# Start of a scan with feed-forward kernel: first unit's decay product moved ahead of the column product, five dummy matmuls left out, constant fills moved, weight block 0 loaded in two parts

## The chip, the core and the metric

The kernel runs on one core of one Trainium2 chip. The metric is the device time of one execution in microseconds; the time before is the median of three runs. A profiled execution has a time of its own, and a span from its first to its last instruction, which is a little shorter.

## What is computed

A state-space scan over 4 batches, 8 heads, 768 positions (head size 32, state size 16), and then a two-layer network over the 3072 tokens that come out of it:

```python
L = np.exp(cum[:, :, :, None] - cum[:, :, None, :]) * causal   # cum: running sum of log a
M = np.einsum('bhin,bhjn->bhij', Cc, Bc) * L
y = einsum(M, xc) + einsum(Cc, state) * np.exp(cum)
state = decay_full * state + sum_j(Bc_j * xc_j * decay_from_j)
...
h = x @ w_in          # 256 -> 2048
out = np.maximum(0.01 * h, h) @ w_out
```

All inputs are float32 and the output is float32.

## The kernel before

**Units.** The positions are cut into 8 chunks of 96 (`Q`). One chunk of one batch is a unit, `u = 4 * chunk + batch`, 32 in all, each with 8 heads. For a unit the kernel needs a decay matrix `lt` (112 rows: 96 positions and 16 rows of the incoming state; 8 heads by 96 columns), the scores `sc` of the unit (C times B), their elementwise product, and then the unit's products: `y` from `lt` and `xs` (line 348) and the new state from `xs` and `bn` (line 357).

**Decay matrices.** Units 0 and 1 (`DIRECT = 2`) get theirs in float32: `decay_mask` (line 239) puts large negative numbers above the diagonal into a PSUM tile `pd`, `decay_direct` (line 246) adds the sums of logarithms from `reach` (filled by GpSimd, line 199) through the matrix `after`, and `decay_of` (line 276, ScalarE) takes the exponential. Units 2 to 15 use a shorter way: the running sums are split into three bfloat16 parts on VectorE (`split_sums`, lines 227 to 230), stored to DRAM (`parts_d`), loaded back as rows of `dl` (line 254) and `dr` (line 257), and `decay_pe` (line 265) makes the matrix with one bfloat16 matmul for each half. `dl` also has rows that are constant: `upto_b` (copied by ScalarE, line 630), ones and zeros (set by VectorE, lines 611 and 612). `dr` is filled by lines 183, 187 and 191.

**Column product.** `columns` (line 217) makes the sums from a position to the chunk's end for all 256 columns of `la`, and ScalarE turns them into `erev` (line 218). `state_decay` (line 303, GpSimd) multiplies `bn` by it, and the state products of line 357 wait for that.

**Scores.** `scores(u)` works in two halves. Each half takes a PSUM tile `sc` of two banks from a pool of two tiles, runs its matmuls (line 321), and VectorE multiplies the result into `lt` (line 326). `columns` uses one of the two tiles of the same pool (`second`), the running sums another (`first`).

**Dummies.** `keep_warm` issues matmuls of an all-zero matrix (line 128) that nothing reads: `WARM = 6` at the start, `WARM2 = 2` behind the masks, `WARM2 = 2` ahead of the first `decay_pe`, and one ahead of each of `scores(2)`, `scores(3)` and `scores(4)`.

**Order.** The instructions of each engine stand in the order in which the program writes them (lines 597 to 689); each engine works in that order and waits on semaphores. The loop of line 638 runs over units 0 to 9: the decay matrix of unit `u + 2`, the scores of unit `u + 1`, the products of unit `u`, with VectorE's difference `xl` (line 391) for each unit behind them, and between them the decoding of weight blocks on ScalarE and VectorE (lines 445, 452, 458, 465, 472). Then the two-layer network begins: `ffn_in` (line 554) and `ffn_out` (line 578) run over 16 blocks of 128 hidden features and tiles of 512 tokens, with the units 10 to 31 put between them.

**Loads.** All loads are issued by SyncE in order, but for the first load of `dr` rows, which ScalarE issues. The order at the start is `la`, `bt`, two of `cc`, `bn`, `xs`, then (as soon as the parts are ready) the store `parts_d`, weight block 0 (`raw`, 512 KB), two loads of `dl` rows, a load of `dr` rows, and the loads of chunk 1.

Of the kernel before, what the change touches and what calls it, by code (L numbers as in the profile page):

```python
# [10 lines left out]
F32 = mybir.dt.float32  # L11
F32R = mybir.dt.float32r
BF16 = mybir.dt.bfloat16
U32 = mybir.dt.uint32
# [4 lines left out]
Q = 96  # L19
NC = S // Q  # L20
QE = Q + N
# [7 lines left out]
B_COLS = NB * QE  # L29
LAG = 3  # L30
WARM = 6
WARM2 = 2
RAWS = 3
SHIFT = 448
LOAD = 4
# [25 lines left out]
BUSY = (17, 21, 25, 30, 34, 38, 42, 46, 50)  # L61
LIGHT = (9, 11, 13, 14, 16)
KD = Q + 3 * NH + 3
MAG_MIN = float(np.uint32(0x38000000).view(np.float32))
MAG_MAX = float(np.uint32(0x47EFFFFF).view(np.float32))

# [2 lines left out]
def scan_ffn(ctx: ExitStack, tc: tile.TileContext, a_l, b_l, c_l, bn_l, x_l, w_l, out_l):  # L69
# [25 lines left out]

    raws, bcs, xss, bns = {}, {}, {}, {}

    def fetch_w(f, eng=nc.sync):
        raws[f] = wr.tile([128, 2 * DM, 2], U32, name="raw")
        eng.dma_start(raws[f].rearrange("p c w -> p (c w)"), w_l[f].bitcast(U32))  # L100

    ccs = [pst.tile([128, 2, NB, Q], F32, name=f"cc{i}") for i in range(2)]

# [99 lines left out]
        )  # L203

    nc.vector.tensor_copy(upto_b, upto)

    erev = const.tile([QE, ncols], F32, name="erev")
    ccol = const.tile([QE, ncols], F32, name="ccol")
# [388 lines left out]
    with tc.tile_pool(name="ps_d", bufs=2, space=PSUM, reuse_waits="tile") as ps_d:  # L597
# [10 lines left out]
        for u in range(DIRECT):  # L608
            fill_reach(u)
        nc.gpsimd.memset(ccs[1], 0.0)  # L610
        nc.vector.memset(dl[Q:], 1.0)
        nc.vector.memset(dl[Q:Q + 3 * NH, :, Q:], 0.0)
        fill_first()
        fill_less()
        prow = first[:, 0, :Q]
        sum_rows(prow, 0)
        split_sums(prow)
        nc.sync.dma_start(parts_d, parts)
        fetch_w(0)
        for u in range(DIRECT):  # L620
            decay_mask(pds[u])
        keep_warm(second[:, 1], WARM2)
        columns(erev, after, AF.Exp, second[:, 0])
        state_decay(0)
        decay_direct(0, pds[0])
        decay_of(0, pds[0])
        fill_slots(1, SLOTS // 2)
        scores(0)
        decay_direct(1, pds[1])
        nc.scalar.copy(dl[:Q], upto_b.unsqueeze(1).to_broadcast([Q, SLOTS, QE]))  # L630
        decay_load(DIRECT, 2, nc.scalar)
        decay_load(DIRECT + 2, SLOTS - 2)
        decay_of(1, pds[1])
        fill_slots(SLOTS // 2, SLOTS)
# [3 lines left out]
        for u in range(FIRST_UNITS):  # L638
            v = u + 2
            if u:  # L640
                decay_pe(v, free_tile())
            if u == 0:
                rest = unit_out(u, free_tile())
                rest()
            if u + 1 < FIRST_UNITS:
                scores(u + 1, int(0 < u < 4))
            else:
                pair_now((), (u + 1, u + 2))
                settle()
                state_decay(3)  # L650
                abs_more()
                pg = ctx.enter_context(tc.tile_pool(name="pg", bufs=LAG + 2))
                ffn_in(0, free_tile()[:, 0])
            if u:
                rest = unit_out(u, free_tile())
                rest()
            else:
                pd = free_tile()
                keep_warm(pd[:, 0], WARM2)
                decay_pe(v, pd)  # L660
            c, b = divmod(u, NB)
            if u == 1:
                fetch_w(1)
            if c + 2 <= 3:
                if b == 2:
                    fetch_bc(c + 2)
                if b == 3:
                    fetch_bn(c + 2)
            if u == 3:
                fetch_x(2)  # L670
            if u == 5:
                fetch_w(2)
            if u == 7:
                alloc_x(3)
                fetch_x(3)
            if u > 7:
                fetch_more()
            if u in (2, 5):
                state_decay(1 if u == 2 else 2)
            if u:  # L680
                settle()
            if u == 1:
                decode_abs(0)
            if u == 4:
                decode_abs(1)
            decode(LEAD.get(u, 0))
# [326 lines left out]
```

## Time and profile before

| What | Value |
|---|---|
| Runs | 318.66, 318.91, 316.94 us; median 318.66 us |
| Profiled execution | 318.41 us, its span 316.7 us |
| TensorE busy | 310.4 us (98%) |
| VectorE busy | 212.0 us (67%) |
| ScalarE busy | 180.7 us (57%) |
| GpSimd busy | 128.5 us (41%) |
| First matmul of the two-layer network (line 554) | starts at 29.24 us |

The profile names the engines PE (TensorE matmul), PEld (its weight loads), DVE (VectorE), ACT (ScalarE), POOL (GpSimd) and SP (SyncE); a `q` behind it is the engine's instruction queue. `L246` is line 246. Times count in us from the span's start. Matmuls are pipelined and their ends are modelled, so that a PE that waits can read as busy: a late start of the next group shows it. A float32 matmul shows as two records.

### The profile page before, as it was taken

The numbers are of one execution on the slowest core, as the hardware profiler recorded it, in microseconds if no ns is written. First come the engines' busy times: TensorE is split into PE (matmuls) and PEld (weight loads), VectorE is DVE, ScalarE is ACT, GpSimd is POOL, SyncE is SP. The second block draws the span as 40 slices with busy tenths as digits, with TensorE's granted clock in tenths as the row PEclk, the third lists the DMA queues.
The fourth block names the chain that finished last, engine by engine and source line by source line (L and its number), as shares of the span: only waits on it lengthen the run. The fifth ranks groups of instructions, "written<-read, shape, count | busy, mean of one in ns | idle before, by whom it ended". The sixth has DMA issues, their size and how long they took to land.

```text
span 316.7 us, 6261 instructions
## 1 busy us (share of the span) xinstructions
PE 310.4 (98%) x2407; PEld 245.8 (78%) x2407; DVE 212.0 (67%) x350; ACT 180.7 (57%) x353; POOL 128.5 (41%) x215
## 2 busy tenths in 40 slices
PE   8999999999999999999999999999999999999995
PEld 4566877777888878888887878788887888888884
DVE  5697787898987677767634444277367676767561
ACT  3776776848574755646454634375365547645551
POOL 6288644614554242724434330070035466335100
PEclk9999999999999999999999999999999999999999
DMA  6987626094518322350204101000001000000003
GB/s 166 253 223 232 173 81 214 23 274 133 155 67 248 108 89 66 96 126 2 90 0 156 66 1 68 0 2 0 0 0 66 2 0 0 2 0 0 2 2 132
DMA packets 11722, 26.29 MB, mean 83 GB/s; under 512 B 2380, under 2 KB 4652, under 8 KB 11692
## 3 DMA queue, kind: packets, MB, share of 16 engines
q1 hardware_dynamic: 11641, 25.88, 27.3%
q8 instruction: 19, 0.31, 0.4%
q14 instruction: 11, 0.09, 0.1%
q10 hardware_dynamic: 51, 0.01, 0.0%
HBM read 22.57 MB, written 3.32 MB: 82 GB/s over the span
## 4 chain that ended last, share of the span: by engine, by line
PE 95%; DVE 2%; ACT 1%; issue 1%; DVEq 0%; ACTq 0%
PE op L578 27%; PE hp L554 26%; PE sc L800 9%; PE op L820 7%; PE sc L820 6%; PE hp L800 3%; PE sc L411 3%; PE sc L348 3%; PE sc L321 2%; PE pd L348 1%; PE pd L265 1%; PE sc L128 1%; PE pd L246 1%; DVE w L465 1%; PE sc L357 1%
## 5 line engine op out<-in xcount | busy, mean ns | idle before, releaser
L567 DVE TENSOR_TENSOR gl<-hp,gh 128x512 fp32r<-128x512 f32 x63 | 43.4, 689 | 55.4 <-ACT hp L564 55.3
L561 ACT ACTIVATE gh<-hp 128x512 fp32r<-128x512 f32 x63 | 37.6, 598 | 63.0 <-PE hp L554 62.9
L578 PE MATMUL op<-gh,wh 128*128 128x512 f32 x128 | 50.9, 398 | 0.0
L554 PE MATMUL hp<-xh,wh 128*128 128x512 f32 x126 | 50.0, 397 | 0.4 <-DVE gl L567 0.4
L578 PE MATMUL op<-gh,wl 128*128 128x512 f32 x128 | 49.9, 390 | 0.0
L578 PE MATMUL op<-gl,wh 128*128 128x512 f32 x128 | 49.8, 389 | 0.0
L554 PE MATMUL hp<-xl,wh 128*128 128x512 f32 x126 | 49.2, 390 | 0.0
L554 PE MATMUL hp<-xh,wl 128*128 128x512 f32 x126 | 49.2, 390 | 0.0
L384 POOL COPY xs<-stage 16x64 f32<-16x64 f32 x112 | 30.8, 275 | 30.5 <-ACT stage L381 25.9
L766 POOL TENSOR_TENSOR sl<-s,sh 128x512 fp32r<-128x512 f32 x8 | 10.4, 1295 | 71.3 <-ACT sh L765 71.3
L564 ACT ACTIVATE hp<-hp 128x512 f32<-128x512 f32 x63 | 37.5, 595 | 0.0
L297 POOL TENSOR_SCALAR_AFFINE_SELECT lt<-lt 96x768 f32<-96x768 f32 x16 | 15.7, 982 | 47.8 <-ACT lt L296 47.8
L288 POOL TENSOR_TENSOR lt<-lt,ccol 112x768 f32<-112x768 f32 x16 | 25.2, 1577 | 10.8 <-DMA lt<-crow_d 6.0
L578 PEld LDWEIGHTS op<-gh,wh 128*128 128x128 f32 x128 | 24.0, 188 | 7.0 <-issue 1.4
L554 PEld LDWEIGHTS hp<-xh,wh 128*128 128x128 f32 x126 | 23.7, 188 | 5.9 <-DVE gl L567 0.8
L578 PEld LDWEIGHTS op<-gl,wh 128*128 128x128 f32 x128 | 24.0, 188 | 5.1
L554 PEld LDWEIGHTS hp<-xl,wh 128*128 128x128 f32 x126 | 23.6, 188 | 5.4 <-DVE xl L391 0.5
L578 PEld LDWEIGHTS op<-gh,wl 128*128 128x128 f32 x128 | 24.0, 188 | 4.6
L554 PEld LDWEIGHTS hp<-xh,wl 128*128 128x128 f32 x126 | 23.7, 188 | 4.8 <-DVE wl L485 0.2
L424 DVE TENSOR_TENSOR lt<-sc,lt 112x384 f32<-112x384 f32 x44 | 21.6, 548 | 3.5 <-ACT xh L386 1.8
L833 DVE TENSOR_TENSOR gl<-c,gh 128x512 fp32r<-128x512 f32 x24 | 23.1, 962 | 1.0 <-ACT c L830 0.7
L829 ACT ACTIVATE gh<-hp 128x512 fp32r<-128x512 f32 x8 | 4.8, 600 | 27.2 <-PE hp L800 27.2
(164 smaller groups left out, 617.0 us busy)
## 6 DMA issues: line engine op xcount, KB each, us to landing
raw<-w_l SPq DMA_DIRECT2D x16, 512.0 KB, 3.3
lt<-crow_d SPq DMA_DIRECT2D x16, 336.0 KB, 4.6
xs<-x_l SPq DMA_DIRECT2D x8, 384.0 KB, 8.2
out_l<-ob SPq DMA_DIRECT2D x12, 256.0 KB, 2.2
bn<-bn_l SPq DMA_DIRECT2D x8, 231.0 KB, 3.8
bt<-b_l SPq DMA_DIRECT2D x8, 224.0 KB, 6.4
cc<-c_l SPq DMA_DIRECT2D x16, 96.0 KB, 4.6
la<-a_l SPq DMA_DIRECT2D x1, 96.0 KB
```

The source lines that it names most:

```text
L288: nc.gpsimd.tensor_tensor(out=lts[u], in0=lts[u], in1=ccol[:, u * NH:(u + 1) * NH].unsqueeze(2).to_broadcast([QE, NH, Q]), op=ALU.subtract,)
L297: nc.gpsimd.affine_select(out=lt[:Q], in_=lt[:Q], pattern=[[0, NH], [1, Q]], compare_op=ALU.is_ge, fill=0.0, base=0, channel_multiplier=-1,)
L384: nc.gpsimd.tensor_copy(to[:, :, hh], stage[hh * D:hh * D + N])
L424: nc.vector.tensor_tensor(out=heads, in0=spaces[half][:QE, :, 2 * Q * e:2 * Q * (e + 1)], in1=heads, op=ALU.mult,)
L554: nc.tensor.matmul(hp, lhsT=w_half[half][:, f, k * 128:(k + 1) * 128], rhs=x[t][:, k, :], start=(n == 0), stop=(n == 5),)
L561: nc.scalar.activation(ghs[s], hp, AF.Prelu, alpha=0.01)
L564: nc.scalar.activation(hps[s], hps[s], AF.Prelu, alpha=0.01)
L567: nc.vector.tensor_tensor(out=gls[s], in0=hps.pop(s), in1=ghs[s], op=ALU.subtract)
L578: nc.tensor.matmul(op, lhsT=w_half[half][:, f, DM + m * 128:DM + (m + 1) * 128], rhs=x, start=(first and i == 0), stop=(last and i == 2),)
L800: nc.tensor.matmul(bank, lhsT=w[h], rhs=x[g], start=start and i == 0, stop=i == 2, skip_group_check=True,)
L820: nc.tensor.matmul(outs[t][m], lhsT=w_half[half][:, f, DM + m * 128:DM + (m + 1) * 128], rhs=x, start=first and i == 0, stop=last and i == 2,)
L833: nc.vector.tensor_tensor(out=gl, in0=g, in1=gh, op=ALU.subtract)
```

## The change

Seven things are edited at the start of the program; from the tenth unit on the program is the same.

1. `decay_direct(0)` and `decay_of(0)` stand right behind the masks, and `columns` behind them; ScalarE's load of `dr` rows is issued between the exponential of unit 0 and `erev`.
2. The two dummies behind the masks, the two ahead of the first `decay_pe` and the one ahead of `scores(4)` are left out.
3. `fill_slots(1, 4)` (VectorE) is written ahead of `decay_direct(0)`.
4. The ones and zeros of `dl` are set ahead of the clamp of `la`; the ones are written as float32 words that hold two bfloat16 ones each, half as many elements.
5. ScalarE's copy of `upto_b` into `dl` is ahead of the exponential of unit 0.
6. Weight block 0 is loaded in two halves of 256 KB, one ahead of the first load of `dl` rows, one behind it.
7. For unit 0, VectorE's difference `xl` (`rest()`) is written behind `scores(1)`; it stood ahead of it.

```diff
-    def fetch_w(f, eng=nc.sync):
-        raws[f] = wr.tile([128, 2 * DM, 2], U32, name="raw")
-        eng.dma_start(raws[f].rearrange("p c w -> p (c w)"), w_l[f].bitcast(U32))
+    def fetch_w(f, half=None):
+        if f not in raws:
+            raws[f] = wr.tile([128, 2 * DM, 2], U32, name="raw")
+        part = slice(0, 2 * DM) if half is None else slice(half * DM, (half + 1) * DM)
+        nc.sync.dma_start(
+            raws[f][:, part].rearrange("p c w -> p (c w)"),
...
     nc.vector.tensor_copy(upto_b, upto)
+    nc.vector.memset(dl[Q:].rearrange("p b j -> p (b j)").bitcast(F32), ONES)
+    nc.vector.memset(dl[Q:Q + 3 * NH, :, Q:], 0.0)
...
         nc.gpsimd.memset(ccs[1], 0.0)
-        nc.vector.memset(dl[Q:], 1.0)
-        nc.vector.memset(dl[Q:Q + 3 * NH, :, Q:], 0.0)
         fill_first()
         fill_less()
+        nc.scalar.copy(dl[:Q], upto_b.unsqueeze(1).to_broadcast([Q, SLOTS, QE]))
         prow = first[:, 0, :Q]
         sum_rows(prow, 0)
         split_sums(prow)
         nc.sync.dma_start(parts_d, parts)
-        fetch_w(0)
+        fetch_w(0, 0)
         for u in range(DIRECT):
             decay_mask(pds[u])
-        keep_warm(second[:, 1], WARM2)
+        fill_slots(1, SLOTS // 2)
+        decay_direct(0, pds[0])
+        decay_of(0, pds[0])
+        decay_load(DIRECT, 2, nc.scalar)
         columns(erev, after, AF.Exp, second[:, 0])
         state_decay(0)
-        decay_direct(0, pds[0])
-        decay_of(0, pds[0])
-        fill_slots(1, SLOTS // 2)
         scores(0)
         decay_direct(1, pds[1])
-        nc.scalar.copy(dl[:Q], upto_b.unsqueeze(1).to_broadcast([Q, SLOTS, QE]))
-        decay_load(DIRECT, 2, nc.scalar)
+        fetch_w(0, 1)
         decay_load(DIRECT + 2, SLOTS - 2)
...
             if u == 0:
                 rest = unit_out(u, free_tile())
-                rest()
             if u + 1 < FIRST_UNITS:
-                scores(u + 1, int(0 < u < 4))
+                scores(u + 1, int(0 < u < 3))
...
             else:
-                pd = free_tile()
-                keep_warm(pd[:, 0], WARM2)
-                decay_pe(v, pd)
+                rest()
+                decay_pe(v, free_tile())
```

**Order on PE around the scores of unit 0.** The first piece is the kernel before, behind the masks; `sc_159` is the tile of the column product, `pd_157` and `pd_158` those of the decays of units 0 and 1, `sc_189` and `sc_193` the two halves of `scores(0)`. What stands in brackets is the engine or load queue on which a row waits.

```order
L128 MATMUL sc_159<-idle_97 128x512
L217 MATMUL sc_159<-la_108,after_122 112x256 [waits Pool_49]
L246 MATMUL pd_157<-lt_127,after_122 112x384 [waits Pool_49]
L321 MATMUL sc_189<-cc0_95,bt_110 112x192 [waits DMAHW2_49,DMAHW1_49,DMAHW3_49,DVE_49,PE_49]
L321 MATMUL sc_193<-cc0_95,bt_110 112x192 [waits Activation_49]
L246 MATMUL pd_158<-lt_128,after_122 112x384 [waits Pool_49]
L348 MATMUL pd_214<-lt_186,xs_114 32x96 [waits DMAHW5_49,DVE_49]
```

The second piece is the same place in the changed kernel (its line 255 is line 246 of before, 226 is 217, 330 is 321, 357 is 348); `sc_190` and `sc_194` are the two halves of `scores(0)`.

```order
L255 MATMUL pd_159<-lt_127,after_122 112x384 [waits Pool_49]
L226 MATMUL sc_161<-la_108,after_122 112x256
L330 MATMUL sc_190<-cc0_95,bt_110 112x192 [waits DMAHW2_49,DMAHW1_49,DMAHW3_49,DVE_49,PE_49]
L330 MATMUL sc_194<-cc0_95,bt_110 112x192 [waits DVE_49]
L255 MATMUL pd_160<-lt_128,after_122 112x384 [waits Pool_49]
L357 MATMUL pd_213<-lt_183,xs_114 32x96 [waits DMAHW5_49,Activation_49]
```

The decay product of unit 0 has moved ahead of the column product. The second half of the scores waited on ACT before (for `erev`, which reads `sc_159`, whose banks `sc_193` takes over); now it waits on DVE, for the multiplication of the first half, because the built program gives `sc_194` the banks of `sc_190`.

**Order on DVE around unit 1.** First the kernel before, from the multiplications of unit 0 on; `pd_214` is the product tile of unit 0, `lt_204` the decay matrix of unit 1.

```order
L326 TENSOR_TENSOR lt_186<-sc_193,lt_186 112x384 [waits PE_49]
L191 COPY dr_126<-dr_126 120x3072
L391 TENSOR_TENSOR xl_232<-pd_214,xh_231 128x2x96 [waits PE_49,Activation_49]
L326 TENSOR_TENSOR lt_204<-sc_241,lt_204 112x384 [waits PE_49]
L326 TENSOR_TENSOR lt_204<-sc_245,lt_204 112x384 [waits PE_49]
```

Then the changed kernel at the same place (its lines 335, 198 and 400 are 326, 191 and 391 of before); `pd_213` is the product tile of unit 0, `lt_203` the decay matrix of unit 1.

```order
L335 TENSOR_TENSOR lt_183<-sc_194,lt_183 112x384 [waits PE_49]
L198 COPY dr_126<-dr_126 120x3072
L335 TENSOR_TENSOR lt_203<-sc_239,lt_203 112x384 [waits PE_49,Activation_49]
L335 TENSOR_TENSOR lt_203<-sc_243,lt_203 112x384 [waits PE_49]
L400 TENSOR_TENSOR xl_231<-pd_213,xh_230 128x2x96 [waits Activation_49]
```

The difference of unit 0 now stands behind both multiplications of unit 1. In both kernels the second `decay_pe` (unit 3) writes into the banks of the product tile of unit 0, and its first matmul waits on DVE for this difference.

**Order on PE ahead of the first `decay_pe`.** The kernel before, from the second half of `scores(1)` to the second `decay_pe`:

```order
L321 MATMUL sc_245<-cc0_95,bt_110 112x192 [waits PE_49]
L128 MATMUL pd_249<-idle_97 128x512 [waits Activation_49]
L265 LDWEIGHTS dl_125 [waits DMAHW0_49]
L265 MATMUL pd_249<-dr_126,dl_125 112x384 [waits DMAHW2_49]
L265 MATMUL pd_256<-dr_126,dl_125 112x384 [waits DVE_49]
L128 MATMUL sc_261<-idle_97 128x512 [waits DVE_49]
```

And the changed kernel (its lines 274 and 135 are 265 and 128 of before):

```order
L330 MATMUL sc_243<-cc0_95,bt_110 112x192 [waits PE_49]
L274 LDWEIGHTS dl_125 [waits DMAHW0_49,DMAHW1_49]
L274 MATMUL pd_248<-dr_126,dl_125 112x384 [waits Activation_49]
L274 MATMUL pd_253<-dr_126,dl_125 112x384 [waits DVE_49]
L135 MATMUL sc_258<-idle_97 128x512 [waits PE_49]
```

The two dummies into `pd_249` are gone; the first `decay_pe` itself now waits for the loads of `dl` and `dr` and, on ACT, for the exponential of unit 1.

More of the change, by code (lines that the diff above doesn't have):

```diff
@@ L31 @@
 WARM = 6
-WARM2 = 2
 RAWS = 3
@@ L63 @@
 KD = Q + 3 * NH + 3
+ONES = float(np.uint32(0x3F803F80).view(np.float32))
 MAG_MIN = float(np.uint32(0x38000000).view(np.float32))
@@ L96, in scan_ffn @@
     raws, bcs, xss, bns = {}, {}, {}, {}
-    def fetch_w(f, eng=nc.sync):
-        raws[f] = wr.tile([128, 2 * DM, 2], U32, name="raw")
-        eng.dma_start(raws[f].rearrange("p c w -> p (c w)"), w_l[f].bitcast(U32))
+    def fetch_w(f, half=None):
[4 more added lines that the diff above has]
+            raws[f][:, part].rearrange("p c w -> p (c w)"),
+            w_l[f].bitcast(U32).rearrange("p (c w) -> p c w", w=2)[:, part].rearrange(
+                "p c w -> p (c w)"
+            ),
+        )
     ccs = [pst.tile([128, 2, NB, Q], F32, name=f"cc{i}") for i in range(2)]
```

## The prediction

> **What bounds the kernel now.** I read the page first (span, chain that ended last), then the busy time by stage, then the timeline of the first 20 us, since only there the program changes. From the page:
>
> ```profile
> span 316.7 us, 6261 instructions
> PE 95%; DVE 2%; ACT 1%; issue 1%; DVEq 0%; ACTq 0%
> ```
>
> The stages (columns: stage, its length, then busy us and instructions of PE, PEld, DVE, ACT and POOL, granted clock, DMA share, GB/s):
>
> ```profile
> 5.00:10.00 5.00, 5.00 (x23) 2.45 (x21) 3.00 (x7) 2.13 (x3) 2.25 (x3) 1.00 0.74 221
> 20.00:25.00 5.00, 4.91 (x97) 3.12 (x96) 4.96 (x14) 4.26 (x11) 4.50 (x11) 1.00 0.78 220
> 30.00:316.70 286.70, 281.85 (x1972) 228.63 (x1971) 189.24 (x294) 161.26 (x313) 108.70 (x162) 1.00 0.23 70
> ```
>
> After 30 us PE is busy 281.85 of 286.7 us and does the same work in both kernels: whatever the start wins or loses is carried to the end as it is. From 20 to 25 us DVE is the full engine too (4.96 of 5 us). In 5 to 10 us PE reads 5.00 of 5, but only 23 instructions: there a late start counts, not the share. So the question is how much sooner or later the first units run. The timeline (start, length, engine, line, tiles, count, idle time before and its releaser):
>
> ```profile
> 4.20 1.49 PE L239 MATMUL pd<-later,upto_b 96*112 96x384 bf16 x4
> 5.48 0.93 PE L128 MATMUL sc<-idle 128*128 128x512 bf16 x2
> 6.24 0.60 PE L217 MATMUL sc<-la,after 96*112 96x256 f32 x2
> 6.68 1.45 PE L246 MATMUL pd<-lt,after 96*112 96x384 f32 x4
> 8.06 0.59 PE L321 MATMUL sc<-cc,bt 32*112 32x192 f32 x8
> 8.16 0.81 ACT L276 ACTIVATE lt<-pd 112x768 f32<-112x768 f32 x1 [0.91 <-PE pd L246]
> 8.58 1.54 PE L246 MATMUL pd<-lt,after 96*112 96x384 f32 x4
> 9.01 1.02 DVE L326 TENSOR_TENSOR lt<-sc,lt 112x384 f32<-112x384 f32 x2 [1.93 <-ACT lt L276]
> 10.16 0.81 ACT L276 ACTIVATE lt<-pd 112x768 f32<-112x768 f32 x1 [0.23 <-PE pd L246]
> 10.65 0.59 PE L321 MATMUL sc<-cc,bt 32*112 32x192 f32 x8
> 11.18 0.60 PE L128 MATMUL pd<-idle 128*128 128x512 bf16 x2
> 11.33 0.36 DVE L391 TENSOR_TENSOR xl<-pd,xh 128x192 fp32r<-128x192 f32 x1 [0.43 <-PE sc L321]
> 11.66 0.81 PE L265 MATMUL pd<-dr,dl 123*112 123x384 bf16 x4
> 12.24 1.51 ACT L276 ACTIVATE lt<-pd 112x768 f32<-112x768 f32 x2 [0.94 <-PE pd L265]
> 12.31 0.38 PE L128 MATMUL sc<-idle 128*128 128x512 bf16 x1
> 12.62 0.64 PE L321 MATMUL sc<-cc,bt 32*112 32x192 f32 x8
> 13.32 1.02 DVE L326 TENSOR_TENSOR lt<-sc,lt 112x384 f32<-112x384 f32 x2 [0.70 <-PE sc L321]
> 13.80 0.50 PE L265 MATMUL pd<-dr,dl 123*112 123x384 bf16 x2
> ```
>
> The reader is to see four things. DVE's first multiplications (9.01) waited 1.93 us for the exponential of unit 0 (8.16 to 8.97), and that for the decay product of line 246, ahead of which stand two dummies and the column product, 5.48 to 6.68. Both halves of `scores(0)` ran together at 8.06, ahead of that exponential. Both `decay_pe` (x4 at 11.66) ran back to back, because unit 0's difference `xl` (11.33) came early. And four masks take 5.48 - 4.20 = 1.28 us, 0.32 each, while four products of the same 384 columns take 12.31 - 11.66 = 0.65, 0.16 each: TensorE runs at half pace first. The dummy pair takes 0.76 (5.48 to 6.24), where a half-paced one takes 0.43 (512 columns against 384) and a full-paced one half of that; so the second dummy is part slow, and the pace doubles near 6.14.
>
> **The change, part by part.** *First unit's decays.* The product now starts at 5.48, 1.20 earlier. Before, the exponential started 8.16 - 6.68 = 1.48 after it. Of the four records one now falls into the slow time and takes 0.64 for 0.32, so it starts at 5.48 + 1.48 + 0.32 = 7.28 and ends at 8.09: 0.88 sooner than 8.97. The column product follows at about 7.18 and takes 0.44 (6.24 to 6.68), so the scores can start at 7.62, not 8.06.
>
> *The halves of the scores.* Here the order turns it round. The second half now goes into the banks of the first, so it waits until DVE has multiplied the first half. From scores to multiplication takes 13.32 - 12.62 = 0.70, so the first multiplication starts at 7.62 + 0.70 = 8.32 (the exponential has ended by then). One takes 0.55:
>
> ```profile
> L326 DVE TENSOR_TENSOR lt<-sc,lt 112x384 f32<-112x384 f32 x20 | 10.2, 550 | 3.0 <-ACT lt L276 1.9 <-PE sc L321 1.1
> 17.25 1.02 DVE L326 TENSOR_TENSOR lt<-sc,lt 112x384 f32<-112x384 f32 x2
> 17.88 1.02 PE L321 MATMUL sc<-cc,bt 32*112 32x192 f32 x8
> 18.18 0.35 DVE L391 TENSOR_TENSOR xl<-pd,xh 128x192 fp32r<-128x192 f32 x1
> ```
>
> In the pair at 17.25 PE resumes on a freed tile 17.88 - 17.80 = 0.08 behind the first multiplication's end. So the second half starts at 8.32 + 0.55 + 0.08 = 8.95. Queued behind it on PE is the decay product of unit 1, 0.52 later (8.06 to 8.58): 9.47, where it was 8.58. **The term is +0.89**: a gain of 0.88 on ScalarE has become a loss of 0.89 on PE. With lags 0.1 shorter in all it would be +0.79.
>
> *The first `decay_pe` and the difference.* With 0.89 added, `scores(1)` starts at 10.65 + 0.89 = 11.54, and the exponential of unit 1 ends at 10.16 + 0.89 + 0.81 = 11.86. The two dummies at 11.18 are gone, 0.48 (to 11.66), so unit 2's `decay_pe` can start at 12.06. But unit 3's waits for unit 0's `xl`, now behind both multiplications of unit 1: these start at 11.54 + 0.70 = 12.24, `xl` 0.93 later (17.25 to 18.18) at 13.17, and ends 0.36 later, 13.53; PE goes on at 13.61. Before, that product started at 11.66 + 0.32 = 11.98. **Lateness now: +1.63**; the 0.48 of the dummies has gone into this wait. Behind it on PE stand `scores(2)` and the products of unit 1, and behind these unit 4's `decay_pe`, 1.82 later as before (11.98 to 13.80), at 15.43; unit 3's exponential, 0.81 long and begun 12.24 - 11.66 = 0.58 behind its product, has ended by 15.0 and does not add. With lags 0.1 shorter at both places the sum is +1.43.
>
> *The dummy ahead of `scores(4)`* (about 0.3 with its change of weights, 12.31 to 12.62 for its like). It gains 0 to 0.3. I take 0.1: the next scores (17.88) are released by DVE's multiplication at 17.25, with DVE full in the stage that follows, so PE would only arrive sooner at that wait.
>
> *Fills and copies.*
>
> ```profile
> 2.81 0.29 DVE L602 TENSOR_SCALAR la<-la 96x256 f32<-96x256 f32 x1 [0.68 <-DMA la<-a_l]
> 3.34 0.81 DVE L611 MEMSET dl<- 32x896 bf16 x1 [0.24 <-issue]
> 4.22 0.11 DVE L612 MEMSET dl<- 24x64 uint32 x1
> 9.00 0.94 ACT L630 COPY dl<-upto_b 96x896 bf16<-96x896 bf16 x1
> ```
>
> DVE waited 0.68 for `la` ahead of the clamp. The memsets go there: 0.40 if the time goes with the elements (448 for 896), with the zeros 0.51; covered. If the ones took their 0.81 still, 0.92 with the zeros, the clamp and all behind would be 0.24 late: bounds 0 to +0.24, I take 0, since it is the same operation on half as many elements. The copy of `upto_b`, 0.94, lies in ScalarE's idle time ahead of 7.28. Taking them out of 3.34 to 4.33 lets the parts end about 0.2 sooner; who waits for them is the next part.
>
> *Loads and `erev`.*
>
> ```profile
> 5.84 0.35 SPq L618 DMA_DIRECT2D parts_d<-parts  x1
> 6.88 0.38 ACT L218 ACTIVATE erev<-sc 112x256 f32<-112x256 f32 x1 [2.47 <-PE sc L217]
> 7.34 1.06 POOL L303 TENSOR_TENSOR bn<-bn,erev 112x512 f32<-112x512 f32 x1 [1.15 <-ACT erev L218]
> 7.78 0.75 SPq L254 DMA_DIRECT2D dl<-parts_d  x2
> 8.23 0.51 ACTq L257 DMA_DIRECT2D dr<-parts_d  x1
> 8.94 0.36 SPq L106 DMA_DIRECT2D bt<-b_l  x1
> ```
>
> SyncE went on at 7.78, when the parts had landed. ScalarE's load of `dr` now waits for that too and not for the exponential, so it is issued near 7.8, 0.4 sooner, and its first user is PE at 12.06, not 11.66: 0.8 more room. `erev` is queued behind this issue on ScalarE: 7.8 + 0.51 = 8.3, ended at 8.7; `state_decay` (1.06) ends at 9.85, and PE needs it for the state products, behind unit 1's decay product (from 9.47, 1.54 long) and before 11.54: covered by about 1. The extra issue on SyncE is about 0.4, so chunk 1's loads are issued from 9.4, not 8.94; their first user, `scores(4)`, stands behind the `decay_pe` that was at 13.80 and is now later. Cost 0 (if ever one landed late, at most these 0.4).
>
> **Sum:** +0.89 + 0.74 (from 0.89 to 1.63) - 0.1 = **+1.5 us** on the profiled execution's 318.41 (span 316.7 and 1.7 around it): 319.9. The median of the runs, 318.66, is 0.25 above that execution; I leave the sum on the profiled one. Own range 319.2 to 320.7.
>
> **Rivals.** (1) *The lead comes through, faster.* The chain of waits shows PE without a gap through this stage:
>
> ```profile
> 5.69 0.72 PE sc L128 x2
> 11.24 0.54 PE pd L128 x2
> 16.15 0.22 PE sc L128
> ```
>
> If it were bound by its own work, each dummy left out would shorten it: 0.72 + 0.54 + 0.22 = 1.48, so 316.9. For it: the chain, and the 1.93 us that DVE waited. Against: the halves share banks. It decides only if the second half can start by 8.06, which needs the first multiplication to end by 7.98, 0.9 before my working has it. (2) *Nothing is left, 318.4.* DVE's full stage could take up the lateness. Against: DVE still waited 0.70 for PE at 13.32, so its queue starts later as a whole; the waits would have to be 1.5 shorter. (3) *The clock falls back, slower.* With the dummies gone PE stands still near 8.2 to 8.95 and 12.4 to 13.6; if that makes it run at half pace again for as long as the first time (from the first dummy to 6.14, about 5 us), half of that time's work is lost, 2.5 more: 318.4 + 1.5 + 2.5 = 322.4. For it: the slow pace at the start is in the rows, and the profile's clock column reads 1.00 in all stages, so it shows no fall beforehand. Against: these are 2.0 us in two pieces, of the 8.1 from 5.48 to 13.6; the rest is work.
>
> [...]
>
> **How the numbers follow.** Forecast 0.62; rival 1 0.14; rival 2 0.16; rival 3 0.08. Predicted 319.9. The range takes in rivals 1 and 2 and the forecast's upper end with both bounds (+0.24 and +0.4) put on: 316.8 to 321.4, leaving out rival 3 and little else. One per cent (3.2 us) is about what a measurement of this kernel can tell from no change. Rival 1 gives 0.5%, so faster by over 1% is 0.02; slower by over 1% is rival 3 with most of its weight, 0.06; within 1% 0.92.
>
> **What would show it.** In the profile after: exponential of unit 0 near 7.3; `scores(0)` in two groups of four, the second near 8.9 and released by DVE; unit 1's decay product near 9.4; two `decay_pe` apart, the second near 13.5 and released by `xl`; the first network matmul 1.2 to 1.7 later than before. It is wrong if both halves run together, if unit 3's `decay_pe` follows unit 2's at once, or if the half pace returns behind 8 us.

## The result and the profile after

| Kernel | Runs | Lowest | Median | Highest |
|---|---|---|---|---|
| before | 20 | 316.86 us | 318.12 us | 319.20 us |
| changed | 20 | 319.29 us | 325.91 us | 329.96 us |

The 20 runs of the changed kernel lie in separate places: seven at 319.29 to 319.96, two at 321.36 and 323.04, eleven at 325.63 to 329.96; one more run on record, 319.38, lies with the seven. The ratio to before is 1.0067, with a 95% interval of 1.0043 to 1.0091; it leaves out the eleven, as runs that lie over 1.5% above the kernel's fastest. The seven have a median of 319.65; forecast was 319.9. But the eleven are more than half, and before never shows such a thing: in the 66 runs that it had beside the experiments on the same chips its highest is 319.46. So the change has two effects: some 1.5 us in its best runs, and 1.7 to 10.3 us more in 13 of the 20. The second is a clock effect wherever a profile or the mean clock tells, the third rival of the prediction, which I had given a chance of 0.08.

The profiled execution of the changed kernel is one of the eleven (326.52 us). Its page and its stages (columns as before: stage, its length, busy us and instructions of PE, PEld, DVE, ACT, POOL, granted clock, DMA share, GB/s):

```profile
span 324.8 us, 6255 instructions
PE 90%; DVE 5%; ACT 2%; issue 1%; POOL 1%; DVEq 0%; ACTq 0%; POOLq 0%
```

```profile
5.00:10.00 5.00, 5.00 (x13) 2.48 (x11) 2.67 (x4) 1.67 (x3) 1.40 (x3) 1.00 0.56 172
20.00:25.00 5.00, 5.00 (x89) 3.03 (x85) 2.68 (x6) 2.41 (x7) 1.35 (x6) 1.00 0.09 17
```

The share of PE on the chain falls from 95% to 90%, and DVE's rises from 2% to 5%. From 5 to 10 us PE is still fully busy, but with 13 instructions instead of 23; and from 20 to 25 us DVE, full before (4.96), has 2.68. PE is busy and gets little done. The timeline of the same execution says why:

```profile
4.31 1.49 PE L248 MATMUL pd<-later,upto_b 96*112 96x384 bf16 x4
5.15 1.04 DVE L238 CAST parts<-rest 128x96 bf16<-128x96 f32 x1
5.38 0.73 POOL L619 MEMSET cc<- 128x768 f32 x1
5.59 2.77 PE L255 MATMUL pd<-lt,after 96*112 96x384 f32 x4
8.40 0.81 ACT L285 ACTIVATE lt<-pd 112x768 f32<-112x768 f32 x1 [2.92 <-PE pd L255]
9.14 0.98 PE L330 MATMUL sc<-cc,bt 32*112 32x192 f32 x4
10.25 0.56 DVE L335 TENSOR_TENSOR lt<-sc,lt 112x384 f32<-112x384 f32 x1 [2.51 <-PE sc L330]
10.86 0.98 PE L330 MATMUL sc<-cc,bt 32*112 32x192 f32 x4 [0.74 <-DVE lt L335]
11.78 2.90 PE L255 MATMUL pd<-lt,after 96*112 96x384 f32 x4
16.55 0.89 PE L274 MATMUL pd<-dr,dl 123*112 123x384 bf16 x2
18.07 0.80 PE L274 MATMUL pd<-dr,dl 123*112 123x384 bf16 x2 [0.63 <-DVE xl L400]
24.10 0.53 PE L274 MATMUL pd<-dr,dl 123*112 123x384 bf16 x2
37.15 0.50 PE L563 MATMUL pd<-xh,wh 128*128 128x512 f32 x1
```

The decay products take 2.77 and 2.90, where before's took 1.45 and 1.54; a `decay_pe` takes 0.89 at 16.55 and 0.53 at 24.10. TensorE ran at half pace until about 24 us, where before had it only to 6.14. The clock column of the stages reads 1.00 all the same: it holds what was recorded, and the first record of this execution is the grant, at 23.75; the half pace ahead of it is seen in the durations only (2.77 and 2.90 for 1.45 and 1.54). The first network matmul comes at 37.15, where it was 29.24: 7.91 later, and the execution is 326.52 - 318.41 = 8.11 longer. So the loss is made at the start and carried to the end, as the prediction had it.

Both predicted waits are there too: `scores(0)` in two groups of four, the second released by DVE (0.74), and two `decay_pe` apart, the second released by `xl` (0.63). To read them at full pace, the changed kernel was profiled once more:

> The changed kernel itself, once more, for a profile in which the clock is granted early. Theory: if it is, exp of unit 0 near 7.3, the second half of scores(0) near 8.95 and released by VectorE, unit 1's decay product near 9.5, unit 3's decay_pe near 13.6 and released by the difference, and a time of 319.3 to 320.0. If the clock is late again: the rows as in the profile after, near 325.9.

This execution took 322.98. Its clock came at 4.06, went at 14.30 and came back at 24.54, so it is at full pace from 4.06 to 14.30:

```profile
4.85 1.45 PE L255 MATMUL pd<-lt,after 96*112 96x384 f32 x4
4.99 1.21 DVE L238 CAST parts<-rest 128x96 bf16<-128x96 f32 x1
6.34 0.81 ACT L285 ACTIVATE lt<-pd 112x768 f32<-112x768 f32 x1 [0.86 <-PE pd L255]
6.40 1.35 DVE L198 COPY dr<-dr 120x2304 bf16<-120x2304 bf16 x1
6.67 0.58 PE L330 MATMUL sc<-cc,bt 32*112 32x192 f32 x4
7.66 0.55 DVE L335 TENSOR_TENSOR lt<-sc,lt 112x384 f32<-112x384 f32 x1
8.26 0.58 PE L330 MATMUL sc<-cc,bt 32*112 32x192 f32 x4 [1.02 <-DVE lt L335]
8.76 0.38 ACT L227 ACTIVATE erev<-sc 112x256 f32<-112x256 f32 x1 [1.60 <-DMA parts_d<-parts]
8.78 1.54 PE L255 MATMUL pd<-lt,after 96*112 96x384 f32 x4
9.22 2.01 POOL L312 TENSOR_TENSOR bn<-bn,erev 112x512 f32<-112x512 f32 x1 [3.10 <-ACT erev L227]
9.37 0.95 DVE L198 COPY dr<-dr 120x3072 bf16<-120x3072 bf16 x1
11.29 0.33 PE L366 MATMUL pd<-xs,bn 96*32 96x32 f32 x16 [0.50 <-POOL bn L312]
11.55 0.59 PE L330 MATMUL sc<-cc,bt 32*112 32x192 f32 x8
12.07 0.53 PE L274 MATMUL pd<-dr,dl 123*112 123x384 bf16 x2
13.58 0.48 PE L274 MATMUL pd<-dr,dl 123*112 123x384 bf16 x2 [0.98 <-DVE xl L400]
```

The two waits are 1.02 and 0.98 at full pace. Unit 3's `decay_pe` starts at 13.58; 13.61 was forecast. There is a third wait that was not forecast: the state products (line 366) wait 0.50 for POOL's state decay. Two things make that late: `erev` starts at 8.76, held through the issue of the load by the landing of `parts`, and the state decay behind it takes 2.01, where it took 1.06 before. With 1.06 it would have ended at 10.28, ahead of 10.79, where the wait begins. No profile was taken of one of the seven low runs; after_again is one of the runs that lost the clock on the way.

### The profile page after: what moved, and what is told of

It is laid out like the page before. It is cut to its first block, busy times and chain, and to the rows that moved or that the text cites. A ratio compares the mean times of both kernels' runs of the same rounds, so it can differ in the third digit from the quotient of the medians.

```text
span 324.8 us, 6255 instructions
## 1 busy us (share of the span) xinstructions
PE 317.4 (98%) x2402; PEld 248.8 (77%) x2402; DVE 213.5 (66%) x350; ACT 180.8 (56%) x353; POOL 128.4 (40%) x215
## 4 chain that ended last, share of the span: by engine, by line
PE 90%; DVE 5%; ACT 2%; issue 1%; POOL 1%; DVEq 0%; ACTq 0%; POOLq 0%
PE op L587 26%; PE hp L563 24%; PE sc L805 9%; PE op L825 7%; PE sc L825 6%; PE hp L805 3%; PE sc L420 3%; PE sc L330 3%; PE sc L357 2%; PE pd L255 2%; PE pd L357 1%; DVE w L474 1%; PE pd L274 1%; PE sc L135 1%; DVE lt L335 1%
```

## The experiments

Theory A: where the clock holds, the loss is the two serial waits. Theory B: the rest of the loss is the clock, which comes late or is taken back because TensorE has too little to do at the start. Rivals: the late clock is the chip's own doing; the loss lies in the loads and fills. All were run in rounds with the kernel before on one chip. "Low group" are the runs of a kernel from its lowest up to the first gap of 0.7 us or more; a ratio is to before, formed like the one above, with its 95% interval.

| Kernel | Runs | Low group | The others |
|---|---|---|---|
| changed | 20 | 7 at 319.29 to 319.96 | 321.36 to 329.96 |
| e1 column product elsewhere | 6 | 1 at 319.3 | 321.75 to 324.36 |
| e2 difference early | 12 | 8 at 318.57 to 319.54 | 4 at 324.53 to 324.97 |
| e3 both | 11 | 3 at 318.66 to 318.83 | 319.6 to 322.92 |
| e4 two dummies back | 11 | 8 at 319.38 to 320.08 | 3 at 323.52 to 324.01 |
| e5 all five dummies back | 6 | 6 at 319.6 to 320.93 | none |
| e6 before without the dummies | 12 | 10 at 316.57 to 318.17 | 319.67, 321.43 |
| e7 dummies in the stops | 6 | 2 at 320.48, 320.64 | 323.12 to 325.36 |
| e8 no serial halves | 9 | 2 at 318.99, 319.0 | 320.29 to 323.99 |
| e9 as e8, `erev` ahead of the load | 6 | 1 at 319.27 | 321.58 to 323.62 |
| e11 as e9, two dummies, fill moved | 8 | 1 at 318.8 | 320.89 to 325.15 |
| e12 before with the masks' dummies only | 12 | 12 at 316.96 to 319.69 | none |

### The two waits, one at a time and together

The column product in free columns of unit 1's decay tile, so that the scores' halves have a tile each (its output is not the reference's, so it serves for times only; no run shows why):

```diff
-        columns(erev, after, AF.Exp, second[:, 0])
+        for g in range(2):
+            nc.tensor.matmul(
+                pds[1][:QE, g, 4 * Q:], lhsT=after, rhs=la[:, g * 128:(g + 1) * 128],
...
+        nc.scalar.activation(
+            erev.rearrange("p (g c) -> p g c", g=2), pds[1][:QE, :, 4 * Q:], AF.Exp
+        )
```

> The changed kernel, but the column product is written into the unused last 128 columns of the two banks of unit 1's decay tile (two matmuls of 128 columns in place of one of 256), so that both halves of the scores of unit 0 find a free pair of banks and the second no longer waits for the multiplication of the first. Unit 1's decay product waits for the reading of that column product instead (about 8.7). Theory A (the changed kernel's own 1.5 to 2 us come from the two serial waits): the two halves run together near 7.6, unit 1's decay product starts near 8.75 and not 9.47, total 0.5 to 0.9 us below the undisturbed runs of the changed kernel (319.3 to 320.0), that is about 319.0. Rival theory (the loads or the clock make the difference): no change, 319.3 to 320.0. On the late clock (about half of the runs of the changed kernel near 326): if the stop between the halves lets the clock stay at half pace, no run above 322; if the missing dummies do, about half of the runs near 325 again.

The difference of unit 0 ahead of `scores(1)` again:

```diff
                 rest = unit_out(u, free_tile())
+                rest()
...
-                rest()
                 decay_pe(v, free_tile())
```

> The changed kernel with the difference of unit 0 written ahead of the scores of unit 1 again, as in the kernel before. Theory A: the second decay product of the bfloat16 way (unit 3) no longer waits for the multiplications of unit 1; it starts near 12.7 and not 13.6, total 0.5 to 0.9 us below the undisturbed runs of the changed kernel (319.3 to 320.0), about 319.0. Rival (loads or clock): no change. Late clock: as many runs near 326 as the changed kernel has (about half), since the stop between the halves and the missing dummies remain.

Both (with the same remark on the output):

> Both of these edits at once on the changed kernel. Theory A: unit 1's decay product near 8.75, unit 3's near 12.0 or below, total 1.3 to 1.9 us below the undisturbed runs of the changed kernel, about 318.0, the time of the kernel before (318.1) or up to 0.5 below it. Rival (loads or clock make the changed kernel's difference): 319.3 to 320.0. Late clock: none if idle TensorE is its cause, about half of the runs near 325 if the missing dummies alone are.

Measured: medians 323.42 (ratio 1.0133, 1.0083 to 1.0183), 319.22 (1.0041, 1.0021 to 1.0061) and 319.96 (1.0088, 1.0056 to 1.0119). Of e1 only one run is low, which prices nothing. In e2 the low group has a median of 319.09, 0.56 below the 319.65 of the change; against the before of its own rounds (317.94, where it was 318.12) that is 0.38. 0.5 to 0.9 was expected of e2, so this wait is real and of about that size or a little less. With both edits the three lowest lie at 318.66 to 318.83, some 0.8 below (0.65 by the before of their own rounds), not the 1.5 that would have been the whole. A reason is in the rows of e3, from an execution of 319.6:

```profile
6.65 0.59 PE L330 MATMUL sc<-cc,bt 32*112 32x192 f32 x8
8.75 0.39 ACT L638 ACTIVATE erev<-pd 112x256 f32<-112x256 f32 x1 [1.62 <-DMA parts_d<-parts]
9.28 1.51 PE L255 MATMUL pd<-lt,after 96*112 96x384 f32 x4 [2.04 <-ACT erev L638]
```

The halves run together at 6.65, as they should, but unit 1's decay product then waits 2.04 for `erev`, whose columns lie in its tile. My edit put one wait in the place of the other, so e1 and e3 don't price the first term. They do show that `erev` stands late.

### Which dummies bring the clock

Two dummies behind the masks again:

```diff
             decay_mask(pds[u])
+        keep_warm(second[:, 1], 2)
```

> The changed kernel with the two dummies behind the masks put back, ahead of unit 0's decay product; both waits remain. If the late clock comes from the missing dense work at 5.5 to 6.2 us: no run above 322, all near 320.0 (0.4 more than the undisturbed runs of the changed kernel, since the dummies take 0.76 us and unit 0's decay product then runs faster). If it comes from idle TensorE at 8 to 14 us: about half of the runs near 326 still.

All five again (besides these, two ahead of the first `decay_pe` and `int(0 < u < 4)` for `scores(4)`):

> The change with all five dummies back: two behind the masks, two ahead of the first decay_pe, one ahead of scores(4). Theory (the clock is granted late, or taken back, because TensorE has too little to do in the first 14 us): no run above 320.5, all near 319.6 to 320.0, since the dummies lie in the stops that the two waits leave; the two dummies behind the masks alone left 3 of 11 runs near 323.8. Rival (idle time behind the halves of the scores takes the clock back, which dummies elsewhere do not fill): some runs stay at 321 to 324. Rival (the late clock is the chip's, not the kernel's): about half of the runs stay near 326.

Three between the halves of `scores(0)` and three ahead of the first `decay_pe`, none behind the masks:

```diff
             sc = score_tile()
+            if u == 0 and half == 1 and 3:
+                keep_warm(second[:, 1], 3)
...
-                decay_pe(v, free_tile())
+                pd = free_tile()
+                keep_warm(pd[:, 0], 3)
+                decay_pe(v, pd)
```

> The change with three dummies between the halves of scores(0) and three ahead of the first decay_pe, none behind the masks: they fill the two stops in which TensorE waits for VectorE. Theory (the clock needs work at 5.5 to 6.2 us to come early, and work in the stops to stay): the runs that begin with a late clock remain, near 325, the ones that had it taken back near 322 are gone, and the rest lie at 319.6 to 320.2. Rival (only the idle time in the stops decides): all runs at 319.6 to 320.2.

The kernel before without the five, and nothing else changed:

```diff
-        keep_warm(second[:, 1], WARM2)
...
-                scores(u + 1, int(0 < u < 4))
+                scores(u + 1, int(0 < u < 3))
...
-                keep_warm(pd[:, 0], WARM2)
```

> The kernel before, less the same five dummies and nothing else: no serial halves, the difference still early. Theory (the late clock comes from the dummies that are missing, whatever the order): a part of the runs at 322 to 326, the others at 317.0 to 317.9, since without the two waits the dummies' time (at most 1.48) is partly won. Rival (the late clock needs the two new waits): all runs between 316.9 and 318.0, none above 319.5.

And with the two behind the masks kept:

> The kernel before, less the dummies ahead of the first decay_pe and ahead of scores(4); the two behind the masks stay. Theory (the two behind the masks bring the early clock): no run above 319.5, where the kernel before without all five had 2 of 12 above. The time: at most 0.6 below before, since unit 3's decay_pe still waits for the difference of unit 0 (to 11.69, where it started at 11.98): 317.4 to 318.0. Rival (dummies later in the start matter as well): some runs at 319.5 to 322.

Measured: e4 319.94 (1.0105, 1.0068 to 1.0143), e5 320.19 (1.0064, 1.0046 to 1.0082), e7 323.12 (1.0129, 1.0093 to 1.0165), e6 317.69 (0.9988, 0.9970 to 1.0007), e12 317.94 (1.0007, 0.9989 to 1.0025).

With the two dummies behind the masks the runs near 326 are gone (0 of 11), and three near 324 stay; these have a mean clock of 0.983 to 0.984, so theirs was taken back. With all five nothing lies above 320.93 (e5), but two runs lie above the 320.5 that the theory set, and three have a mean clock of 0.993 to 0.994: the profiled one lost the clock for one step, from 11.39 to 14.80. In the stops alone the dummies do not help: four of six are at 323.1 to 325.4, three of them with the clock taken back (0.988 to 0.989), which the theory had excluded. So the late clock belongs to the kernel, not to the chip, and the masks' dummies are a part of what the change misses; e11 below has them too and is late all the same. But theory B as I had put it for e6, that the missing dummies are enough whatever the order, fell: before without them keeps ten of twelve runs at 316.57 to 318.17, and with the masks' two (e12) all twelve but one lie below 319.1. The one, 319.69, is above the 319.5 that e12's theory set; one of twelve there and two of twelve in e6 do not tell the two kernels apart. In before's order TensorE goes on nearly without a stop, by the profiles (busy 3.12 us or more of each 3.41 in e6 from 5.01 to 15.25); in the change's order it stops (waits of 1.02, 0.50 and 0.98 in after_again).

The times of the grants fit a part for the dummies. In four profiles that show more than one change of the clock, the changes lie a multiple of 3.41 apart: 4.06, 14.30 and 24.54 in after_again, 4.57, 11.39 and 14.80 in e5, 4.04, 10.86 and 14.28 in e3, 3.79 and 10.62 in e1. I read that as a grid of such steps with an offset of its own in each execution, and count its points in the other profiles in steps of 3.41 from the change that they show; these points are an estimate. Where one fell between 3.70 and 5.01 us, the clock was granted there in every kernel (e1, e3, e5, e6, e8, e12, after_again). Where one fell at 6.10 to 6.69 instead, the clock was granted there in before (6.14) and e4 (6.15), whose dummies lie right ahead of it (5.48 and 5.61), and not in the changed kernel, e2, e7, e9 and e11; there it came one step later (9.53 in e11) or more (23.75 in the change). The changed kernel shows both: granted at 4.06 in after_again, not at 6.69 in its first profile, five steps ahead of 23.75. But there is one profile for each of the other kernels, and no run sets the offset, so the part of the dummies in this is argued and not shown.

What takes the clock back is read from the stretches between grid points (same columns as the stages). First of after_again, the one that ends where the clock was taken back, and the next, at half pace:

```profile
10.89:14.30 3.41, 2.04 (x33) 1.12 (x33) 1.29 (x3) 1.66 (x5) 1.27 (x5) 1.00 0.97 259
14.30:17.71 3.41, 3.41 (x47) 2.05 (x51) 1.38 (x3) 2.12 (x5) 0.93 (x4) 0.50 0.75 215
```

Of e5, the one that ends where the clock was taken back:

```profile
7.98:11.39 3.41, 2.21 (x20) 1.12 (x24) 1.98 (x3) 0.50 (x2) 1.06 (x1) 1.00 0.68 187
```

Of e3, likewise:

```profile
7.45:10.86 3.41, 1.58 (x12) 0.76 (x16) 2.09 (x4) 0.41 (x2) 1.23 (x1) 1.00 0.64 190
```

And two of e8, in which the clock held from 3.70 to the end:

```profile
7.11:10.53 3.42, 2.20 (x22) 0.88 (x20) 2.46 (x4) 1.08 (x2) 1.31 (x1) 1.00 0.60 169
10.53:13.94 3.41, 2.38 (x35) 1.37 (x37) 1.35 (x4) 1.40 (x4) 1.90 (x5) 1.00 0.92 235
```

The clock was taken back behind stretches in which PE was busy 1.34 (e1, 7.21 to 10.62), 1.58 (e3), 2.04 (after_again) and 2.21 (e5) of 3.41 us, and kept behind 2.20 and 2.38 (e8), 2.52 (after_again, 7.48 to 10.89) and 2.57 (e4, 12.97 to 16.38). As 2.21 lost it and 2.20 kept it, the busy share in these profiles does not part the two, and where a bound lies is open. No stretch was idle as a whole; the longest single wait in them was 2.10 (e1). In before no such stretch exists (PE is busy 3.38 to 3.41 in all four up to 16.4 us).

### Where the first wait went: `erev`

Each half of `scores(0)` in a tile of its own, the column product behind both in free columns of the second, the difference early, no dummy:

```diff
-        columns(erev, after, AF.Exp, second[:, 0])
-        state_decay(0)
-        scores(0)
+        first_scores()
...
+    def first_scores():
+        lt = lts[0].rearrange("p (g h) i -> p g (h i)", h=2)
+        tiles = [score_tile() for _ in range(2)]
...
+        columns(erev, after, AF.Exp, tiles[1][:, 0, TS // 2:])
+        state_decay(0)
+        for half, sc in enumerate(tiles):
...
```

> The change without its two waits: the column product of erev stands behind both halves of scores(0), in free columns of the second half's tile, so that each half has a tile of its own and neither waits for the other's multiplication, and unit 0's difference stands ahead of scores(1); no dummy added. Theory (the two waits are the whole of the 1.6 that the change loses where the clock holds): the lowest group of runs at 317.0 to 318.2, at or below the kernel before; a part of the runs still 3 to 7 above it for the late clock, as the dummies are gone. Rival (the loss has another source, such as the loads or the fills): the lowest group stays at 319 or above.

Measured 321.86 (1.0096, 1.0066 to 1.0127), the two lowest at 318.99 and 319.0. Theory A would have them at 317.0 to 318.2: it falls, as far as it took the two waits for the whole, and the rival's 319, with another source of the loss, is what came. The profiled execution of e8 is one of the two, with the clock from 3.70 to the end:

```profile
6.14 0.59 PE L343 MATMUL sc<-cc,bt 32*112 32x192 f32 x8
7.18 1.45 PE L255 MATMUL pd<-lt,after 96*112 96x384 f32 x4
8.75 0.38 ACT L227 ACTIVATE erev<-sc 112x256 f32<-112x256 f32 x1 [1.69 <-PE pd L255]
9.21 2.29 POOL L312 TENSOR_TENSOR bn<-bn,erev 112x512 f32<-112x512 f32 x1 [3.10 <-ACT erev L227]
11.55 0.33 PE L382 MATMUL pd<-xs,bn 96*32 96x32 f32 x16 [1.41 <-POOL bn L312]
12.34 0.98 PE L274 MATMUL pd<-dr,dl 123*112 123x384 bf16 x4
```

Unit 1's decay product starts at 7.18, 1.4 earlier than before's; then everything waits for the state decay (1.41 at 11.55). In e6, which has before's order and neither the serial halves nor the five dummies, `erev` stands at 5.84 and both `decay_pe` at 10.51. The change put ScalarE's load of `dr` ahead of `erev`, and that load was issued at 8.20 only, when `parts` had landed. So with the serial halves gone the next wait is this one. But `erev` is not the whole of it: the state decay takes 2.29 here. With the 1.06 of before it would have ended at 10.27, 0.13 behind the 10.14 at which the wait begins. In the change as it stands it is mostly covered by the serial halves: the prediction's "covered by about 1" was true of that order only.

The load behind `erev` (an edit of e8), then also two dummies behind the masks and the fill of the second C block moved ahead of the masks' fills on POOL:

```diff
+        first_scores()
         decay_load(DIRECT, 2, nc.scalar)
-        first_scores()
```

> The run before this one that had no serial halves (each half of scores(0) in a tile of its own, the column product behind them, the difference early, no dummies), with ScalarE's load of dr moved behind erev. In that run erev stood at 8.75, held by the landing of parts at 8.20 through the load's issue; the state products waited 1.41 for the state decay behind it. Theory (a third wait, the one that I had taken as covered, ate what the two others gave back): erev near 7.1 to 7.5, the state products without a wait, the difference near 10.5 instead of 12.42, and the lowest group of runs at 317.0 to 317.8 instead of 319.0. Rival (the lateness of erev is covered and the loss lies elsewhere): the lowest group stays at 318.8 or above. A part of the runs 2 to 6 above the lowest group for the late clock either way.

```diff
+        nc.gpsimd.memset(ccs[1], 0.0)
         for u in range(DIRECT):
             fill_reach(u)
-        nc.gpsimd.memset(ccs[1], 0.0)
...
+        keep_warm(score_tile()[:, 1], 2)
```

> The same, with two dummies behind the masks again and the fill of the second C block moved on POOL ahead of the masks' fills, into its idle time before la. Theory: the third cast of parts, which took 1.04 while that fill ran on POOL, takes about 0.3, parts is stored about 0.7 sooner, and the clock is granted near 6 in nearly every run, so the median lies at 317.0 to 318.0, at or below the kernel before. Rival (the late clock comes from the order of the change and not from the dummies): runs at 321 to 326 remain, a third of them or more. Rival (the cast is slow for another reason): it stays near 1.0.

Measured: e9 322.2 (1.0134, 1.0100 to 1.0167), e11 324.25 (1.0094, 1.0045 to 1.0143). Neither came out as I expected. By the numbers both rivals hold: e9's lowest is 319.27, above the 318.8 that its rival set, and six of e11's eight runs lie at 322.75 to 325.15, where its rival had a third or more. In e9's profile the clock came at 19.75, in e11's at 9.53, so neither tells what `erev` is worth at full pace from the start; only that, to go by the times, nearly all their runs had a late clock, with two dummies behind the masks too. In e11 these dummies start at 5.89, not at 5.61 as in e4, since the moved fill holds up the clamp of `la` by 0.30: 0.2 us of them are left ahead of the grid point estimated at 6.12. That fits the reading above, but was not tried by itself. Two things in e11 are plain: the cast and the state decay.

```profile
2.64 0.74 POOL L632 MEMSET cc<- 128x768 f32 x1
2.93 0.59 DVE L627 TENSOR_SCALAR la<-la 96x256 f32<-96x256 f32 x1
5.44 0.36 DVE L238 CAST parts<-rest 128x96 bf16<-128x96 f32 x1
10.70 0.38 ACT L227 ACTIVATE erev<-sc 112x256 f32<-112x256 f32 x1 [0.34 <-PE sc L226]
11.17 2.29 POOL L312 TENSOR_TENSOR bn<-bn,erev 112x512 f32<-112x512 f32 x1 [5.43 <-ACT erev L227]
13.51 0.33 PE L382 MATMUL pd<-xs,bn 96*32 96x32 f32 x16 [1.09 <-POOL bn L312]
```

The cast takes 0.36, where it took 1.04 in the profile of the change, and the clamp, now beside the fill, takes 0.59 for 0.29. In these two profiles the stall lies where the fill lies. And `erev` no longer waits for the load, only for its own product (0.34), at full pace; the state products wait 1.09 for the state decay all the same, since it takes 2.29. With 1.06 it would have ended at 12.23, ahead of 12.42, where the wait begins. So moving the load alone does not remove this wait: the length of the state decay has its own part in it.

No version beats both kernels: e6 has a ratio of 0.9988, with 1 inside its interval.

## Why the prediction was right, and where it was not

**Right in the sum, for the low runs.** +1.5 was forecast; the seven low runs have 319.65 to 318.12, +1.53. That their clock came early and held is inferred from their times and mean clocks (0.998 to 1.0). The nearest profile at the forecast's clock is e4, whose clock came at 6.15 as before's did at 6.14:

```profile
5.61 0.87 PE L135 MATMUL sc<-idle 128*128 128x512 bf16 x2
9.19 0.58 PE L330 MATMUL sc<-cc,bt 32*112 32x192 f32 x4 [0.48 <-ACT erev L227]
30.47 0.50 PE L563 MATMUL pd<-xh,wh 128*128 128x512 f32 x1
```

The first network matmul stands 1.23 later than before; 1.2 to 1.7 was forecast. But e4 has two dummies more, and its second half of the scores waits for `erev` and not for the first multiplication: this agreement is of the size, not of the path.

**The halves of the scores.** Place and releaser were right. The step from unit 0's decay product to the second half was put at 8.95 - 5.48 = 3.47; after_again has 8.26 - 4.85 = 3.41. The way there was another: the exponential came 0.3 sooner at full pace, but the multiplication came 0.99 behind its scores, not 0.70, as DVE was on the copy of line 198 from 6.40 until 7.75. What this term of +0.89 is worth alone was not priced, since each edit that freed the halves ran into `erev`.

**The difference and unit 3's `decay_pe`.** Right in place, releaser and size: from `scores(1)` to unit 3's `decay_pe` forecast 13.61 - 11.54 = 2.07, measured 13.58 - 11.55 = 2.03. The sum's 0.74 for it is what the wait adds beyond the 0.48 won by the two dummies, so it is not what e2 must give back: by the prediction's working an early difference would end at 12.58 (11.54 + 0.68 + 0.36) and release unit 3 at 12.66, 0.95 sooner. e2 gave back 0.38 to 0.56.

**Fills, copies and loads: wrong, at little cost here.** The memsets ahead of the clamp were put at 0 (bounds 0 to 0.24); the clamp starts at 2.92 instead of 2.81, 0.11 late. "Lets the parts end about 0.2 sooner" failed: `parts` was stored at 6.50, not at 5.84 as before. The first cast waited 1.08 for its sums and came 0.08 sooner only. The third cast takes 1.04, where it took 0.31: it ends at 6.19, just behind POOL's fill (5.38 to 6.11). In before it slipped in ahead of that fill:

```profile
5.21 0.31 DVE L229 CAST parts<-rest 128x96 bf16<-128x96 f32 x1
5.41 0.79 POOL L610 MEMSET cc<- 128x768 f32 x1
```

With the fill moved away in e11 the cast took 0.36, and the clamp beside the fill 0.59 for 0.29: in these profiles DVE's operations take longer beside the fill. In the change, though, the cast is shown to start first (5.15 against 5.38) and ends last, as in before it started first and took 0.31; no run explains the difference. So ScalarE could issue the load of `dr` at 8.19 only, not near 7.8, and `erev` stood at 8.76 (8.3 forecast; both in after_again). The state decay took 2.01 there, not 1.06: 0.95 more, the length of the DVE copy at 9.37 beside it. The cover of about 1 became a wait of 0.50. (In e4, where no copy ran beside it, it took 1.06 and ended at 10.28, 1.25 ahead of its use at 11.53: there the cover was as forecast.) Against it stood a clock that came 2 us sooner (4.06 for 6.14) and brought unit 1's decay product to 8.78, where 9.47 was forecast. These two nearly cancel, so the agreement at 13.58 is partly luck.

**The clock: the step that failed.** Rival 3 had 0.08, and a price of 2.5. Of the 22 runs of the changed kernel (the 20, the one more, after_again) fourteen are above the low group. Four had the clock taken back, by the mean granted clock: 321.36 (mean clock 0.995), 322.98 and 323.04 (0.984), 325.63 (0.968); of these the one with a profile was without it from 14.30 to 24.54, and lies 3.3 above the low group's 319.65. The other ten, 326.20 to 329.96, have a mean of 0.997 to 0.999, too high for even one step of 3.41 at half pace (0.995). One of them is profiled and has the late grant; for the other nine it is inferred from that, and nothing tells why two lie near 330. Their median of 326.55 is 6.9 above. By the prediction's own sign, "if the half pace returns behind 8 us", after_again speaks against it: there it returned at 14.30. Two thoughts led astray. I took the clock's grant at 6.14 as a fixed time that the change leaves alone, and reckoned with its falling back only; but the dummies that were dropped stood right ahead of it. And I took "2.0 us in two pieces" for too little to matter, an estimate that no row of before showed; in after_again the clock was taken back behind a stretch of 3.41 with 1.37 idle (2.04 busy).

**The range.** 316.8 to 321.4 holds the low group, and not the median of all 20 runs, 325.91. Whoever wants to know what the kernel does in use must take that: with the clock the change loses 2.4% in the median.

**Still open.** Why before's order keeps the clock without the dummies in ten of twelve runs and the changed order does not; what the 0.7 or more of the 1.5 that e3 didn't give back consists of, beyond `erev` and the longer state decay; what the halves of the scores cost alone; what takes the clock back, if not the busy share; and why the cast, which starts ahead of the fill, ends behind it.

## What to carry to other kernels

Dummy matmuls may be more than time: eleven of the 20 runs of the change lay above 325, and with two dummies put back none of 11 (e4). Before one is dropped, look where the clock is granted, in more than one profile, and what TensorE does just ahead of it. A wait that is removed shows the next one, here an activation queued behind a DMA issue (`erev` at 8.75 in e8), and a multiplication on POOL that takes 2.01 to 2.29 for 1.06: check what stands in the queue ahead of it, and what runs beside it, before the gain is booked. And look at the spread of the runs, not at the median alone, when a change touches the first microseconds.

## What the runs showed of the hardware

- In four profiles that show more than one change of the clock (after_again, e5, e3, e1), the changes lie a multiple of 3.41 us apart, at other times in each: on 4.06, off 14.30, on 24.54 in after_again; on 4.57, off 11.39, on 14.80 in e5.
- The clock was taken back behind stretches with PE busy 1.34 to 2.21 of 3.41 us (e1, e3, after_again, e5), and kept behind others with 2.20 to 2.57 (e8, after_again, e4): in these profiles no single bound on this share parts the two.
- In the profile of the change the clock column reads 1.00 over the 23.75 us ahead of the first record, in which four decay records took 2.77 where before's took 1.45.
- The bf16 cast on DVE took 1.04 beside a fill on POOL (the change), 0.36 with the fill moved away (e11); POOL's multiplication took 1.06 where no DVE copy ran beside it (e4) and 2.01 beside a DVE copy of 0.95 (after_again).
